# Interleaving three output rows over the quarters of w2, and loading w1's first quarter in two halves

## The chip, the cores and the metric

The kernel runs on one core of one Trainium2 chip. The metric is the time of one execution on the device, in microseconds (us). Three runs of the kernel before gave 223.17, 225.45 and 226.80 us; the median is 225.45 us. One further execution was profiled.

## The reference, cut to what matters

Two blocks follow each other: a linear attention with a decay per head, and a mixer with a low-rank product and a two-layer MLP.

```
gamma = 1.0 - 2.0 ** (-5.0 - np.arange(H))
for t in range(S):
    state = gamma[None, :, None, None] * state + np.einsum('bhd,bhe->bhde', k[:, :, t], v[:, :, t])
    y[:, :, t] = scale * np.einsum('bhd,bhde->bhe', q[:, :, t], state)
...
xt = x.transpose(0, 2, 1)
h = xt @ U @ V
u = x + h.transpose(0, 2, 1)
ch = np.maximum(u @ w_ch1, 0.0) @ w_ch2
return (u + ch)
```

There are 4 batches, 8 heads of 64 values, 768 positions. x, the attention's output with the heads side by side, is 768 x 512 per batch; U is 768 x 32, V 32 x 768, w_ch1 ("w1") 512 x 2048, w_ch2 ("w2") 2048 x 512. Inputs and output are float32; the kernel computes its matrix products in bfloat16.

## The kernel before, in words

**Attention.** A batch's 768 positions are cut into six chunks of 128. For batches 1 to 3 a chunk ci takes these steps: the input tiles of k, q and v are cast (and q and v scaled) to bfloat16 (`prep`, L207, and `prep_q1`, L198); k and q are transposed; `score` (L279) multiplies them into R[ci % 2], a tile of two PSUM banks, and DVE masks both banks (L287); `mix` (L292) multiplies the masked scores with v, adds the product of q with the state so far, ACT evacuates that (x, L308), and the state is brought up to date and evacuated (nsz, L322). Batch 0 has code of its own that runs in two groups of four heads (`STEPS`, L525), an order written out by hand over all engines.

**Mixer.** For each batch, `up` (L425) makes sixteen pieces of relu(u @ w1) for positions 0 to 511, `up_two` (L440) eight pieces for the rest, and `down` (L455) the product with w2: six output rows j of 128 positions, four pieces each (m0 = 0, 4, 8, 12), and a piece needs one quarter of w2. That is 48 pieces in a batch, all counted by the planner at the same cost, 0.864. A row's four pieces add up in one PSUM bank, and after the fourth DVE adds u and the row goes to a store, issued by POOL.

**PSUM.** Eight banks: R[0] and R[1] with two each, one called st, and three called mlp, which are handed out in turn by `bank("mlp")` to whatever asks: an up piece, a down row, a transpose. Who takes a bank waits until the one who had it three calls earlier has been evacuated.

**Order.** `weave` (L486) emits a batch's pieces one after another, and before a piece all the marks whose place (a fraction of the batch's 48 pieces) has come. A mark is a step of the next batch's attention or of a low-rank product: `mark(at, f, ...)` (L798). The places for batch 1 stand in the table AT (L788) and the loop after it. Each engine then runs its own instructions in that order, and an instruction that waits holds up all behind it on its engine. With the places of the kernel before, batch 1's steps fall as follows among batch 0's pieces, counted from 0 (24 is the first down piece, j=0 m0=0):

| before piece | what |
|---|---|
| 23 | `turn_k1` (L255) of chunks 0, 1 |
| 25 | casts of k chunks 2, 3 on ACT; `turn_q1` (L264) of 0, 1 |
| 28 | `score` 0, 1 |
| 29 / 30 | `turn_k1` 2, 3 / `mix` 0 |
| 31 / 32 | `turn_q1` 2, 3 / `mix` 1 |
| 33 | `score` 2, 3 |
| 36 / 37 / 38 | `mix` 2 / `turn_q1` 4, 5 / `mix` 3 |
| 39 | `score` 4, 5 |
| 41 / 43 | `mix` 4 / `mix` 5 |
| 44 / 46 | `lr_proj_turn` (L374) / `lr_uT` (L389) |

`turn_k1` and `turn_q1` transpose on TensorE through an mlp bank; ACT evacuates k, ACT and DVE in turn q. `lr_proj_turn` begins with 24 small products over all six x of the batch, in order of j.

**Loads.** SP issues the loads of k, q and v. POOL issues the weights: w1 in four quarters of 512 columns (`load_w1`, L228), w2 in four quarters (`load_w2`, L233). Both queues share the DMA engines. In the step list, `w0` and `w1` issue w1's first and second quarter; the third is issued after the list (L772), then a tiny copy waits for the first quarter (`feed_behind(511)`, L774) and lets SP go on with q and v of chunks 0 and 1, then w1's last quarter and all four quarters of w2 are issued, and a copy behind w1's second quarter (L779) lets SP go on with chunks 2 to 5. POOL then clears three tiles and casts k, q and v of chunks 0 and 1 (L782).

**The first up pieces.** The step `B1`, `B2` (L742) begins up pieces 0 and 1 with the first two and the third of four rows of w1 (c = 0, 1 and 2), as the transposed u arrives row by row; `up` then adds c = 3.

Of the kernel before, what the change touches and what calls it, by code (L numbers as in the profile page):

```python
# [16 lines left out]
def kernel(  # L17
# [12 lines left out]
    P = 128  # L30
# [193 lines left out]
    def prep_two(nm, pp, eng="P"):  # L224
        for ci in (2 * pp, 2 * pp + 1):
            prep(nm, 1, ci, eng)

    def load_w1(lo, n):  # L228
        nc.gpsimd.dma_start(
            out=w1b[:, :, ds(lo, n)],  # L230
            in_=moe_w_ch1[:, ds(lo, n)].rearrange("(c p) n -> p c n", p=P))

    def load_w2(j):  # L233
        nc.gpsimd.dma_start(
# [20 lines left out]
    def turn_k1(ci):  # L255
        t = bts["k", 1, ci] = rpre.tile([P, 4, P], bf16, tag="kT", name=f"kT_1_{ci}",
                                        bufs=3)
        tp = bank("mlp")
        for hp in range(4):
            nc.tensor.matmul(tp[:, ts(hp, P)], pre["k", 1, ci][:, ds(2 * hp, 2)], ident,  # L260
                             start=True, stop=True)
        evac("A", t.rearrange("p n m -> p (n m)"), tp)

    def turn_q1(ci):  # L264
        g, pp = ci % 2, ci // 2
        if g == 0:
            t = rpre.tile([P, 4, 2 * P], bf16, tag="qT1", name=f"qT_1_{pp}", bufs=2)
            bts["q", 1, ci], bts["q", 1, ci + 1] = t[:, :, :P], t[:, :, P:]
            bts["q1", pp] = t
        src, t = pre.pop(("q", 1, ci)), bts["q1", pp]  # L270
        tp = bank("mlp")
        for n in range(2):
            for j in range(2):
                nc.tensor.matmul(tp[:, ts(2 * n + j, P)], src[:, j, ds(2 * n, 2)], ident,
                                 start=True, stop=True)
        evac("AD"[g], t[:, ds(2 * g, 2)].rearrange("p n (t j) -> p n j t", j=2),
             tp.rearrange("p (n j t) -> p n j t", n=2, j=2))
# [135 lines left out]
    def mlp_pieces(b):  # L413
        gT = gtp.tile([P, NM, S], bf16, tag="gT", name=f"gT_{b}")
        pieces = []
        n = [0]

        def relu(dst, src):
            n[0] += 1
            if n[0] % 3 == 0:  # L420
                nc.vector.tensor_relu(dst, src)  # L421
            else:
                nc.scalar.activation(dst, src, AF.Relu)  # L423

        def up(m, lo, sz):  # L425
            def f():
                g_p = begun.pop((b, m, lo), None)
                c0 = 3 if g_p is not None else 0
                if not c0:
                    g_p = bank("mlp")  # L430
                for c in range(c0, NCB):
                    nc.tensor.matmul(g_p[:, :sz], w1b[:, c, ts(m, P)],  # L432
                                     uTs[b][:, c, ds(lo, sz)], start=(c == 0),
                                     stop=(c == NCB - 1))
                relu(gT[:, m, ds(lo, sz)], g_p[:, :sz])
            return f

        for m in range(NM):
            pieces.append((0.864, up(m, 0, LO)))
        def up_two(m):  # L440
            def f():
                g_p = bank("mlp")
                for n in range(2):
                    for c in range(NCB):
                        nc.tensor.matmul(g_p[:, ts(n, S - LO)], w1b[:, c, ts(m + n, P)],  # L445
                                         uTs[b][:, c, LO:], start=(c == 0),
                                         stop=(c == NCB - 1))
                relu(gT[:, ds(m, 2), LO:], g_p.rearrange("p (n t) -> p n t", n=2))
            return f

        for m in range(0, NM, 2):
            pieces.append((0.864, up_two(m)))
        hold = {}

        def down(j, m0, n0=0, nn=DM):  # L455
            def f():
                if m0 == 0:
                    hold[j, n0] = bank("mlp")
                ch = hold[j, n0]
                for m in range(m0, m0 + 4):  # L460
                    nc.tensor.matmul(ch[:, :nn], gT[:, m, ts(j, P)],  # L461
                                     w2b[:, m, ds(n0, nn)],
                                     start=(m == 0), stop=(m == NM - 1))
                if m0 == NM - 4:
                    o_sb = outp.tile([P, DM], fp32, tag="o_sb",
                                     name=f"o_{b}_{j}_{n0}")[:, :nn]
                    n = ds(n0, nn)
                    nc.vector.tensor_tensor(o_sb, ch[:, :nn], us[b][:, j, n],  # L468
                                            op=ALU.add)
                    if (b, j) == (B - 1, NCK - 1):  # L470
                        nc.sync.dma_start(out=out[b, ts(j, P), n], in_=o_sb)
                    else:
                        stores.append((nc.gpsimd, out[b, ts(j, P), n], o_sb))
            return f

        for j in range(NCK):
            if (b, j) == (B - 1, NCK - 1):
                for n0, nn in ((0, 384), (384, 128)):
                    for m0 in range(0, NM, 4):
                        pieces.append((0.864 * nn / DM, down(j, m0, n0, nn)))  # L480
                continue
            for m0 in range(0, NM, 4):
                pieces.append((0.864, down(j, m0)))
        return pieces
# [204 lines left out]
    def step(s):  # L689
# [15 lines left out]
        if nm in ("K", "Q", "V"):  # L705
            if eng == "S":
                cast_unit("v", u, "P", 0, 2)
            else:
                cast_unit(nm.lower(), u, eng)
        elif nm == "W":  # L710
            cast_unit("v", u, "D", 2, 2)
        elif nm in ("Tk", "Tq"):
            turn_unit(nm[1], u)
        elif nm in ("kT", "qT"):
            turned_unit(nm[0], u, eng)
        elif nm == "S":
            score_unit(u)
        elif nm == "m":
            mask_unit(u)
        elif nm == "ST":  # L720
            state_unit(u, int(at[2]))
        elif nm == "s":
            state_out(u, int(at[2]), eng)
        elif nm == "M":
            mix_unit(u)
        elif nm == "N":
            query_unit(u, False)
        elif nm == "x":
            x_out(u, eng)
        elif nm == "Ub":  # L730
            evac("A", Ub, Uf)
        elif nm == "xt":
            x_turn(u)
        elif nm == "P":
            proj(u, range(NCK if u == 0 else 4))
        elif nm == "R":
            proj(1, range(4, NCK))
        elif nm == "pc":
            pc_out(u // 2, BY["pc"][u // 2])
        elif nm == "E":  # L740
            expand((0, 1) if u == 0 else (u,))
        elif nm == "B":  # L742
            for m in range(2):
                begin_up(m, (0, 1) if u == 1 else (2,))
        elif nm == "u":
            evac(eng, uTs[0][:, u, :LO], xT[u][:, :LO])
        elif nm == "w":
            if u == 0:
                nc.gpsimd.tensor_copy(out=gate0, in_=ready["q", 5][:1, :1])
            load_w1(512 * u, 512)  # L750
        else:
            raise ValueError(s)

# [15 lines left out]

    n_open[0] = 2  # L770
    feed_more()
    load_w1(1024, 512)  # L772
    n_open[0] = 6
    feed_behind(511)  # L774
    n_open[0] = 3 * NCK
    load_w1(1536, 512)
    for j in range(4):
        load_w2(j)
    feed_behind(1023)  # L779
    for t in nsz:  # L780
        nc.gpsimd.memset(t, 0.0)
    for nm in "kqv":  # L782
        prep_two(nm, 0)

    AT = {1: ((0.565, 0.685, 0.80), None, (0.045, 0.09), (0.10, 0.045), None),  # L788
          2: (0.215, 0.185, (0.05, 0.095), (-0.03, 0.0, 0.05, 0.12, 0.39, 0.45),
              (-0.07, -0.035, 0.0, 0.045, 0.36, 0.42)),  # L790
          3: (0.20, 0.20, (0.05, 0.095), (0.01, 0.055, 0.21, 0.255, 0.41, 0.455),
# [13 lines left out]
    for b in range(1, B):  # L805
        s0, step, dm, dt, at_prep = AT[b]
        for ci in range(NCK):
            pair_at = b - 1 + (s0[ci // 2] if b == 1 else s0 + step * (ci // 2))
            if b == 1:
                if ci < NCK - 2:  # L810
                    mark(pair_at - dt[0], turn_k1, ci)
                else:
                    mark(0.671, turn_dma, "k", b, ci)
                mark(pair_at - dt[1], turn_q1, ci)
            else:
                mark(b - 1 + at_prep[ci], prep_chunk, b, ci)
                mark(b - 1 + dt[ci], turn_chunk, b, ci)
            mark(pair_at, score, b, ci)
            mark(pair_at + dm[ci % 2], mix, b, ci)
        if b == 1:  # L820
            for nm, eng, at in (("k", "AP", (0.51, 0.635)), ("q", "PP", (0.54, 0.67)),
                                ("v", "PP", (0.58, 0.70))):
                for pp in (1, 2):
                    mark(at[pp - 1], prep_two, nm, pp, eng[pp - 1])
            mark(0.905, lr_open, b)
            mark(0.905, lr_proj_turn, b)
            mark(0.94, lr_uT, b)
            mark(1.11, lr_expand, b, 0, 4)
        else:
            l0, l1, l2, l3 = LR  # L830
# [43 lines left out]
```

## Time and profile before

| | us |
|---|---|
| median of three runs (lowest, highest) | 225.45 (223.17, 226.80) |
| the profiled execution's own time | 224.14 |
| its span in the trace | 222.3 |
| PE (TensorE matmul) busy | 213.4 (96%) |
| DVE / ACT / POOL busy | 96.7 / 80.7 / 79.7 |
| DMA, queue of SP / of POOL, share of 16 engines | 51.0% / 18.6% |

The span covers the recorded instructions; the execution's own time is 1.84 us longer. PE is busy in nearly the whole span, and the TensorE clock that was granted was 0.998 of full speed. Times below are places in the span. Batch 0's attention and low-rank product fill the first 25 us, its up pieces go from 26 to 49 us, its down pieces with batch 1's attention between them from 49 to 79.5 us.

### The profile page before, as it was taken

How to read it: one execution, taken by the hardware profiler on the slowest of the kernel's cores; microseconds unless marked ns; L12 is line 12 of the kernel's file. 1: busy time of each engine (PE TensorE's matmuls, PEld its weight loads, DVE VectorE, ACT ScalarE, POOL GpSimd, SP SyncE). 2: the span in 40 equal slices, each digit the busy share in tenths (PEclk: the TensorE clock that was granted, in tenths of full speed). 3: DMA queues.
4: the chain of work that ended last, by engine and by line, in shares of the span. 5: the costliest groups of instructions: out<-in, count | busy, mean ns of one | idle time of the engine just before them, and what ended most of it. 6: DMA issues, size and time to landing. Idle time of an engine off the chain costs nothing.

```text
span 222.3 us, 4695 instructions
## 1 busy us (share of the span) xinstructions
PE 213.4 (96%) x1940; PEld 121.9 (55%) x1966; DVE 96.7 (43%) x137; ACT 80.7 (36%) x154; POOL 79.7 (36%) x114
## 2 busy tenths in 40 slices
PE   7999799998999999999999999999999999999993
PEld 2567344774655544578454444587454444774442
DVE  6678546225465176526336144443525242222121
ACT  3676264453734134565030034746030044430000
POOL 5588383012980496036100498053101000000110
PEclk9999999999999999999999999999999999999999
DMA  5999999997899995389899745399113450001212
GB/s 168 330 294 235 192 198 205 195 205 195 214 248 272 272 234 116 75 191 167 181 284 275 182 121 95 82 262 108 47 50 95 141 97 2 0 3 47 92 49 94
DMA packets 91556, 35.10 MB, mean 158 GB/s; under 512 B 73392, under 2 KB 90032, under 8 KB 91536
## 3 DMA queue, kind: packets, MB, share of 16 engines
q1 hardware_dynamic: 85472, 24.59, 51.0%
q0 software_dynamic: 6064, 10.23, 18.6%
q8 instruction: 15, 0.25, 0.5%
q14 instruction: 5, 0.04, 0.1%
HBM read 27.46 MB, written 6.29 MB: 152 GB/s over the span
## 4 chain that ended last, share of the span: by engine, by line
PE 74%; DMA 15%; SPq 7%; issue 1%; POOL 1%; ACT 1%; DVE 0%
PE mlp L461 36%; PE mlp L432 19%; PE mlp L445 10%; DMA in<-in_q_dram 7%; DMA in<-in_k_dram 5%; SPq L106 5%; DMA w1b<-in_moe_w_ch_dram 4%; PE r L284 2%; PE r L305 2%; PE st L316 2%; PE r L300 2%; SPq L137 1%; PE r L347 1%; POOL qp L83 0%; PE r L385 0%
## 5 line engine op out<-in xcount | busy, mean ns | idle before, releaser
L461 PE MATMUL mlp<-w2b,gT 128*128 128x512 bf16 (+2 forms) x384 | 85.9, 370 | 0.9 <-issue 0.2
L423 ACT ACTIVATE gT<-mlp 128x512 bf16<-128x512 f32 x64 | 38.1, 597 | 72.2 <-PE mlp L432 59.1
L461 PEld LDWEIGHTS <-gT 128*128 128x128 bf16 x400 | 37.0, 98 | 39.0 <-issue 0.2
L432 PE MATMUL mlp<-uT,w1b 128*128 128x512 bf16 x244 | 56.3, 379 | 0.3
L411 POOL DMA_DIRECT2D out_dram<-o x23 | 12.8, 556 | 86.8 <-DVE o L468 81.0
L421 DVE TENSOR_SCALAR gT<-mlp 128x512 bf16<-128x512 f32 x32 | 22.1, 689 | 43.5 <-PE mlp L432 22.8
L432 PEld LDWEIGHTS <-w1b 128*128 128x128 bf16 x250 | 23.6, 98 | 27.2
L468 DVE TENSOR_TENSOR o<-mlp,u 128x512 f32<-128x512 f32 (+2 forms) x25 | 16.7, 670 | 44.5 <-PE mlp L461 43.8
L445 PE MATMUL mlp<-uT,w1b 128*128 128x256 bf16 x256 | 29.4, 273 | 0.2 <-ACT gT L423 0.2
L445 PEld LDWEIGHTS <-w1b 128*128 128x128 bf16 x256 | 24.8, 98 | 4.2 <-issue 0.4
L287 DVE TENSOR_TENSOR a<-r,mask 128x1024 bf16<-128x1024 f32 x18 | 21.2, 1219 | 9.5 <-PE r L284 9.5
L83 POOL TENSOR_TENSOR vd<-in,gk 128x512 bf16<-128x512 f32 x18 | 18.7, 1042 | 12.5 <-DMA in<-in_v_dram 7.7
L70 ACT ACTIVATE x<-r 128x512 bf16<-128x512 f32 x20 | 11.9, 596 | 27.3 <-PE r L305 27.0
L81 POOL CAST kd<-in 128x512 bf16<-128x512 f32 x16 | 9.7, 613 | 19.3 <-DMA in<-in_k_dram 19.3
L354 DVE TENSOR_TENSOR u<-r,x 128x512 bf16<-128x512 f32 (+1 forms) x16 | 14.5, 951 | 4.6 <-PE r L347 4.6
L83 POOL TENSOR_TENSOR qd<-in,gq 128x512 bf16<-128x512 f32 x12 | 12.5, 1042 | 1.4 <-DMA in<-in_q_dram 1.4
L70 ACT ACTIVATE nsz<-st 64x256 bf16<-64x256 f32 x30 | 11.2, 372 | 0.3
L83 POOL TENSOR_TENSOR qp<-in,gq 128x512 bf16<-128x512 f32 x6 | 6.2, 1052 | 6.9 <-DMA in<-in_q_dram 6.8
L594 DVE TENSOR_TENSOR a<-r,mask 128x1024 bf16<-128x1024 f32 x6 | 7.3, 1221 | 2.6 <-PE r L587 2.6
L305 PE MATMUL r<-vd,a 128*128 128x64 bf16 x144 | 7.1, 193 | 0.0
L305 PEld LDWEIGHTS <-a 128*128 128x128 bf16 x144 | 6.0, 98 | 0.7
L284 PEld LDWEIGHTS <-kT 64*128 64x128 bf16 x144 | 4.1, 94 | 3.9 <-issue 3.7
(109 smaller groups left out, 147.7 us busy)
## 6 DMA issues: line engine op xcount, KB each, us to landing
in<-in_k_dram SPq DMA_DIRECT2D x24, 256.0 KB, 4.5
in<-in_q_dram SPq DMA_DIRECT2D x24, 256.0 KB, 4.4
in<-in_v_dram SPq DMA_DIRECT2D x24, 256.0 KB, 4.7
out_dram<-o POOLq DMA_DIRECT2D x23, 256.0 KB, 2.5
w1b<-in_moe_w_ch_dram POOLq DMA_DIRECT2D x4, 512.0 KB, 9.2
w2b<-in_moe_w_ch_dram POOLq DMA_DIRECT2D x4, 512.0 KB, 17.2
kT<-kd SPq DMA_TRANSPOSE x14, 3.7
uT<-u SPq DMA_TRANSPOSE x14, 2.4
```

What stands on the lines that cost most here:

```text
L70: nc.scalar.activation(dst, src, AF.Copy)
L83: e.tensor_tensor(dst, src, scale, op=ALU.mult)
L287: nc.vector.tensor_tensor(a, r.rearrange("p i (n m) -> p i n m", n=4), mask[:, None, None, :].to_broadcast([P, 2, 4, P]), op=ALU.mult)
L305: nc.tensor.matmul(o[:, ts(h, D)], a[:, i, hp], vb[:, h], start=(ci == 0 and h == 0), stop=True, skip_group_check=True)
L354: nc.vector.tensor_tensor(v4(us[b][:, ds(j0, nj), e]), R[g][:, :, :nj * P].rearrange("p c (j e) -> p c j e", j=nj), v4(xs[b][:, ds(j0, nj) ...
L411: eng.dma_start(out=dst, in_=src)
L421: nc.vector.tensor_relu(dst, src)
L423: nc.scalar.activation(dst, src, AF.Relu)
L432: nc.tensor.matmul(g_p[:, :sz], w1b[:, c, ts(m, P)], uTs[b][:, c, ds(lo, sz)], start=(c == 0), stop=(c == NCB - 1))
L445: nc.tensor.matmul(g_p[:, ts(n, S - LO)], w1b[:, c, ts(m + n, P)], uTs[b][:, c, LO:], start=(c == 0), stop=(c == NCB - 1))
L461: nc.tensor.matmul(ch[:, :nn], gT[:, m, ts(j, P)], w2b[:, m, ds(n0, nn)], start=(m == 0), stop=(m == NM - 1))
L468: nc.vector.tensor_tensor(o_sb, ch[:, :nn], us[b][:, j, n], op=ALU.add)
```

## The change

Four things are changed, and the marks are placed anew.

- Batch 0's first three output rows run side by side: j = 0, 1, 2 at m0 = 0, then the three at m0 = 4, and so on. The later rows and the other batches keep their order. Each of the three holds an mlp bank until the fourth quarter.
- `turn_k1` and `turn_q1` use the second bank of R[ci % 2] in place of an mlp bank.
- w1's first quarter is loaded in two halves (rows c = 0, 1 and c = 2, 3) at the places of `w0` and `w1` in the step list; the second quarter is issued after the list, ahead of the third. The steps `B1`, `B2` begin three up pieces in place of two.
- w2's last quarter is issued behind the cast of v's chunk 0.

```
-    def load_w1(lo, n):
+    def load_w1(lo, n, c=0, nc_=NCB):
         nc.gpsimd.dma_start(
-            out=w1b[:, :, ds(lo, n)],
-            in_=moe_w_ch1[:, ds(lo, n)].rearrange("(c p) n -> p c n", p=P))
+            out=w1b[:, ds(c, nc_), ds(lo, n)],
+            in_=moe_w_ch1[ds(P * c, P * nc_), ds(lo, n)].rearrange(
+                "(c p) n -> p c n", p=P))
...
     def turn_k1(ci):
-        tp = bank("mlp")
+        tp = R[ci % 2][:, 1]
...
     def turn_q1(ci):
-        tp = bank("mlp")
+        tp = R[g][:, 1]
...
-        for j in range(NCK):
+        side = 3 if b == 0 else 1
+        for m0 in range(0, NM, 4):
+            pieces += [(0.864, down(j, m0)) for j in range(side)]
+        for j in range(side, NCK):
...
         elif nm == "B":
-            for m in range(2):
+            for m in range(3):
                 begin_up(m, (0, 1) if u == 1 else (2,))
...
-            load_w1(512 * u, 512)
+            load_w1(0, 512, 2 * u, 2)
...
     n_open[0] = 2
     feed_more()
+    load_w1(512, 512)
     load_w1(1024, 512)
...
-    for j in range(4):
+    for j in range(3):
         load_w2(j)
     feed_behind(1023)
...
-    for nm in "kqv":
+    for nm in "kq":
         prep_two(nm, 0)
+    prep("v", 1, 0)
+    load_w2(3)
+    prep("v", 1, 1)
...
-    AT = {1: ((0.565, 0.685, 0.80), None, (0.045, 0.09), (0.10, 0.045), None),
+    AT = {1: ((0.565, 0.69, 0.81), None, (0.045, 0.09),
+              (0.465, 0.465, 0.63, 0.642, None, None, 0.52, 0.52, 0.662, 0.662, 0.78, 0.78),
+              None),
...
-                    mark(pair_at - dt[0], turn_k1, ci)
+                    mark(dt[ci], turn_k1, ci)
...
-                mark(pair_at - dt[1], turn_q1, ci)
+                mark(dt[NCK + ci], turn_q1, ci)
...
-            for nm, eng, at in (("k", "AP", (0.51, 0.635)), ("q", "PP", (0.54, 0.67)),
+            for nm, eng, at in (("k", "AP", (0.535, 0.635)), ("q", "PP", (0.54, 0.67)),
...
-            mark(0.905, lr_open, b)
-            mark(0.905, lr_proj_turn, b)
-            mark(0.94, lr_uT, b)
+            mark(0.915, lr_open, b)
+            mark(0.915, lr_proj_turn, b)
+            mark(0.948, lr_uT, b)
```

With the new places the table above becomes: the casts of k chunks 2, 3 on ACT come before piece 26, behind `turn_q1` 0, 1; `turn_k1` 2, 3 before piece 31; `mix` 1 and then `turn_q1` 2, 3 before piece 32; `score` 2, 3 before piece 34; `mix` 3 and right after it `turn_q1` 4, 5 before piece 38; `mix` 4 before piece 42; `mix` 5 and right after it `lr_proj_turn` before piece 44. The others stay where they were.

## The prediction, on record before the result

> **What bounds the kernel now.** I read the page first, then TensorE's waits, then the busy time by stretch, then the timelines of TensorE and ACT around the waits, and last the weight queue in windows of 1 us.
>
> The page, part 1, engines:
> ```profile
> PE 213.4 (96%) x1940; PEld 121.9 (55%) x1966; DVE 96.7 (43%) x137; ACT 80.7 (36%) x154; POOL 79.7 (36%) x114
> ```
> The waits of PE:
> ```profile
> PE mlp L756 <- DVE zeros L152: 1.2, 1, 1.2
> PE mlp L403 <- DMA w1b<-in_moe_w_ch_dram: 1.1, 1, 1.1
> ...
> PE r L284 <- ACT qT L70: 0.5, 1, 0.5
> PE mlp L445 <- ACT gT L423: 0.2, 1, 0.2
> ```
> Busy time by stretch (stretch, its length, then PE and PEld busy, and so on), cut at these waits:
> ```profile
> 24.97:26.05 1.08, 0.00 (x2) 0.01 (x1) 1.04 (x2) 0.00 (x0) 0.00 (x0) 1.00 1.20 198
> 26.05:47.81 21.76, 21.66 (x158) 12.87 (x161) 8.54 (x12) 10.17 (x17) 9.62 (x15) 1.00 1.20 201
> 47.81:48.05 0.24, 0.00 (x1) 0.00 (x0) 0.00 (x0) 0.24 (x2) 0.00 (x0) 1.00 1.22 250
> 48.05:52.99 4.94, 4.88 (x31) 2.77 (x32) 1.43 (x2) 2.36 (x5) 1.04 (x1) 1.00 0.76 191
> 52.99:53.50 0.51, 0.00 (x1) 0.02 (x2) 0.48 (x1) 0.46 (x1) 0.00 (x0) 1.00 1.20 287
> ```
> The reader is to see that TensorE is the bound from 25 us to the end. In the stretch that the change touches it stands still three times: 1.08 us before the first up piece (for w1's first quarter), 0.24 us at the last up piece (an mlp bank whose relu is not out), 0.51 us before score 0. Their sum, 1.83 us, is all that this execution has to give; the work on TensorE is the same before and after. Why score 0 waits stands in ACT's timeline (start, length):
> ```profile
> 51.36 0.63 ACT L77 ACTIVATE kd<-in 128x512 bf16<-128x512 f32 x1 [2.38 <-DMA in<-in_k_dram]
> 52.19 0.63 ACT L77 ACTIVATE kd<-in 128x512 bf16<-128x512 f32 x1 [0.20 <-DMA in<-in_k_dram]
> 52.72 0.72 ACT L70 ACTIVATE qT<-mlp 128x512 bf16<-128x512 f32 x1
> ...
> 56.67 0.60 ACT L70 ACTIVATE x<-r 128x512 bf16<-128x512 f32 x1 [0.17 <-PE r L305]
> 57.16 0.77 ACT L70 ACTIVATE nsz<-st 64x256 bf16<-64x256 f32 x2
> 57.98 0.75 ACT L70 ACTIVATE qT<-mlp 128x512 bf16<-128x512 f32 x1
> ```
> q's evacuation stands behind two casts that wait for k's loads of chunks 2 and 3.
>
> **w1's first quarter in two, a third piece begun.** The weight queue (q0), windows 20:21, 23:24 and 25:26 (packets, MB):
> ```profile
> q0 software_dynamic: 44, 0.05, 57.8%
> ...
> q0 software_dynamic: 168, 0.16, 121.8%
> ...
> q0 software_dynamic: 192, 0.19, 117.7%
> ```
> With the windows between (0.16, 0.17, 0.19) the queue has moved 0.5 MB, one quarter, at about 23.8 us; the first quarter landed at 26.0 (issue 18.05 plus 8.0), so 2.2 us behind. The second landed at 28.5 (19.53 plus 9.0), 2.1 us behind its own 1.0 MB. A first half (0.25 MB at about 22.2) should land near 24.4. TensorE is done with the step before at 24.97, and both evacuations on ACT end at 24.44, so B1 starts at 25.00: a gain of 1.05 us. Its six matmuls (0.216 us each, from 0.86 for four) end at 26.30; the second half, at 26.0, is then there.
>
> A late wait follows it. Piece 3 takes piece 0's bank. B2 (three) ends at 26.95, pieces 0 to 2 need one matmul each and the expansion 0.23: 27.82. Relu 0 starts 0.19 after its matmul's end (27.16, the distance seen before), takes 0.60, and 0.06 passes to TensorE: 28.01. A new wait of 0.19. Net here: -0.86. From both sides: -1.3 at most (the six matmuls of B1 run inside the wait if all w1 is late), and +0.2 if the first half lands no sooner than the quarter does.
>
> w1's second quarter goes from 19.53 to 21.30 in POOL's stream: it is moved past the cast of v5 (1.06). It is needed at piece 4, at 28.87 by the sum above. In the queue's order it stands behind the same bytes as before, and these run out at 23.8; from issue to first packet the first quarter took 2.3 us (18.05 to about 20.4), so the second has packets from 23.6. I take 28.5, no wait. The other end: it lands later by the whole 1.77, at 30.3, a wait of 1.5. The third quarter's issue moves from 21.30 to about 22.1; it stands behind the same bytes and landed at 31.4, needed at 33: nothing. The copy that lets SP go on still waits for the landing at 26.0.
>
> One rule of the Trainium skill speaks against the halves: "DMA: Bandwidth & Descriptors", section "Anatomy of one DMA — SWDGE (gpsimd) path", gives each DMA a fixed cost of about 2 us, most of it the receipt of the last byte. If the halves paid it one after the other, the second would land near 28 us, B2 would wait 1.7 us, and the whole sum would come to about +1.3. The second quarter, landing 2.5 us behind the first at 0.2 MB in a us, shows no such addition; the rival by it is worked out from rows below.
>
> **The turns in R.** The mlp bank that the last up piece waited for is no longer taken by a turn: -0.24. The turns need R free: chunks 2 and 3 turn before piece 31, a mix and a piece behind the masks of 0 and 1 (1.22 each, done before mix 0 and 1): nothing. If the cover were gone, a mask is 1.22. During pieces 24 to 35 no other step asks for an mlp bank; the fourth row takes row 0's, whose add (0.69) is done 2 us earlier.
>
> **The casts of k on ACT behind qT.** They leave qT's way: score 0, now at about 51.5 in place of 53.5, finds q evacuated at 49.5: -0.51. The casts still end at 52.8; next on ACT is x of mix 0, at about 54.3, and turn_k1 2 needs them at 55.3: 1.5 and 2.5 us of cover.
>
> **w2's last quarter.** POOL issues it behind the cast of v 0 (landed 44.6, cast to 45.7); it is moved past a gate, three clears, two casts of k, two of q and one of v, and 0.77 us of issue goes ahead of v 1's cast, which waits for its load until 50.3 anyway. The queue is still at w2's third quarter then (landed 46.9), so it lands at 50 to 52; first needed at piece 33, near 58.6. Nothing; 6 us of cover. The loads of k, q, v share the engines with it for as long as before. q 2 and 3 are cast by 57.1, and turn_q1 3 comes at about 57.5: 0.4 us of cover, then us for us (taken 0, ends -0 and +0.7, by the 1.1 that a late first packet could shift).
>
> **Two steps set closer.** Mix 3 is now followed at once by turn_q1 4, 5, one piece and score 4. On ACT, from mix 0 above: 1.69 us from mix's L305 (56.24) to the end of nsz (57.93), then q's evacuation, 0.70, and 0.06. TensorE gets from L305 to score in 0.23 + 0.22 + 0.45 + 0.86 = 1.76, ACT in 2.45: +0.69 (0 to 0.9). Mix 5 is followed at once by lr_proj_turn: x needs 0.80 from the end of L305 and 0.06, the products of rows 0 to 4 take 5/6 of 0.45: +0.49 (0 to 0.6). Score 2: mask 2 starts behind row 0's add, ending at about 61.6 where mix 2 comes at 61.8: 0 (to 0.3).
>
> Three stores come together, on POOL behind the casts of q and v 4, 5 (about 65.8, landing 2.5 later), with three output buffers: row 3's add, at 68.4, just finds one. An add held up there costs nothing until its bank is wanted five pieces on.
>
> **Sum.** -0.86 - 0.24 - 0.51 + 0.69 + 0.49 = -0.43 us. On the profiled execution, 224.14 (span 222.3 and 1.84 around it), that is 223.7. That execution lies 1.3 below the median, 225.45, between the lowest and the highest; the three runs lie 3.6 us apart, so 2% (4.5 us) is about what a measurement of this kernel can tell from no change.
>
> **Rivals.**
> - w1's second quarter is late and TensorE waits at piece 4: 1.5 us, net +1.05, 225.2. This is the one on the other side; it decides from a landing after 29.3 (28.87 plus 0.43). For it: only 0.2 us of bytes are left in the queue when its packets come. Against: the queue has bytes. 0.17.
> - The second half pays a fixed part of its own: the smallest transfer in the list of DMA issues (64 KB) takes 1.6 us, so 27.6 and a wait of 1.3 in B2: net +0.87, 225.0. Against: the spacing of the quarters. 0.08. By the Trainium skill's figure its wait would be 1.7.
> - The first half lands no sooner than the whole: the halving doesn't do what it says, net +0.6, 224.8. Against: the queue is in order. 0.10.
> - The two new waits on ACT are hidden: net -1.6, 222.5. For: both rest on distances of 0.06 to 0.2 us read from one execution. 0.13.
> - q's loads late for turn_q1 3, 0.7 of wait: 224.4. 0.07.
> - Over 2% slower: several waits at once, above all w1 or q by 4 us and more: 0.07. Over 2% faster: 1.83 us of waits do not hold 4.5; only if the median's runs wait more for loads than the profiled one: 0.05.
>
> **How the numbers follow.** My forecast has 0.33. Its own range is 223 to 224.6. With the rivals, 222.5 to 225.2, and the spread of the runs around them (223.17 to 226.80 before) the range is 221.8 to 226.7. All cases but the last two lie within 2% of 225.45: 0.88 the same, 0.05 faster, 0.07 slower.
>
> **What would show it.** Right: B1 starting near 25.0 with no wait on w1b, no wait at L445 and at score 0, new waits of PE on ACT qT at score 4 and on ACT x at the products of lr_proj_turn, and a relu's bank at piece 3. Wrong: a wait on w1b at L432 (piece 4), on w1b at B2, on POOL qp at a turn, or a longer stretch between 80 us and the end, which the change should leave at its length.

## The result, and the profile after

The changed kernel takes 225.49 us (median of 20 runs, 223.89 to 228.53), the kernel before 224.10 us (20 runs). The ratio is 1.0063, with a 95% interval of 1.0041 to 1.0085: about 1.4 us slower, within the 2% either way. The forecast was 223.7 us, 0.43 us less than the profiled execution of the kernel before, so the sign was wrong.

The first profile of the changed kernel fell in a disturbed execution (227.84 us); the readings below are from a second one, 225.56 us with a span of 223.8, called as_changed. Its page, engines:

```profile
PE 215.9 (96%) x1966; PEld 122.2 (55%) x1966; DVE 96.5 (43%) x137; ACT 80.6 (36%) x154; POOL 80.6 (36%) x115
```
The waits of its PE:
```profile
PE mlp L433 <- DMA w1b<-in_moe_w_ch_dram: 1.4, 1, 1.4
...
PE r L275 <- ACT x L70: 0.5, 2, 0.2
PE mlp L379 <- ACT x L70: 0.3, 1, 0.3
...
PE r L285 <- ACT qT L70: 0.2, 1, 0.2
```
The three waits that the prediction counted (w1 before the first up piece, gT at the last, qT at score 0) are gone. In their place stand w1 again, now at up piece 4 (L433), x twice at a turn of q (L275), x at lr_proj_turn (L379), and qT at a later score. Busy time by stretch (stretch, length, PE, PEld and so on), cut at the first up matmul, piece 4, the first down piece, score 0 and batch 1's first up piece:

```profile
25.03:28.87 3.84, 3.84 (x26) 1.51 (x24) 2.33 (x4) 1.09 (x2) 3.03 (x5) 1.00 1.11 172
28.87:30.43 1.56, 0.20 (x2) 0.01 (x1) 0.85 (x2) 0.60 (x1) 0.06 (x1) 1.00 1.20 209
30.43:49.12 18.69, 18.69 (x145) 11.99 (x145) 6.41 (x8) 9.20 (x16) 7.41 (x11) 1.00 1.12 198
49.12:53.11 3.99, 3.99 (x26) 1.92 (x23) 1.42 (x2) 2.19 (x4) 0.18 (x1) 1.00 1.11 198
53.11:80.95 27.84, 26.74 (x286) 15.57 (x285) 13.12 (x15) 10.37 (x21) 16.68 (x21) 1.00 1.04 252
```
B1 starts at 25.03 (the forecast said 25.00), but TensorE stands still from 28.87 to 30.43. The last stretch, from score 0 to batch 1's first up piece, takes 27.84 us. The same stretch in the profile before:

```profile
53.50:79.51 26.01, 25.75 (x280) 15.17 (x285) 12.84 (x15) 10.39 (x21) 15.62 (x20) 1.00 1.00 244
```
It took 26.01 us there, 1.83 less.

The best tool of this study came out of this: TensorE's timeline, cut at five fixed points. Each stretch has the same work in every version, so its length differs by waits alone. All numbers are start times from that timeline, or differences of them, in us. (lr_turn is the first transpose of batch 0's u among the up pieces, L368 before and L369 after; lines of the changed kernel lie one to five further down.)

| profile | B1 starts | B1 to lr_turn | to first down piece | to score 0 | to batch 1's first up | rest |
|---|---|---|---|---|---|---|
| before, as shown | 26.05 | 4.65 | 18.22 | 4.58 | 26.01 | 142.8 |
| before_look | 26.45 | 4.66 | 18.21 | 4.49 | 26.01 | 142.9 |
| before_look2 | 26.00 | 4.79 | 18.21 | 4.00 | 26.00 | 142.9 |
| before_look3 | 25.39 | 4.66 | 18.22 | 4.01 | 26.01 | 142.9 |
| as_changed | 25.03 | 6.27 | 17.82 | 3.99 | 27.84 | 142.9 |
| changed_look | 25.06 | 5.57 | 17.82 | 4.00 | 27.83 | 142.9 |

Two columns hardly move between executions of one kernel but differ between the two kernels: to the first down piece (-0.40 with the change) and from score 0 on (+1.83). The rest, behind the change, hardly moves at all. The three others move with loads.

### The profile page after: what moved, and what is told of

Read it like the earlier page. It is cut to its first block, busy times and chain, and to the rows that moved or that the text cites. A ratio compares the mean times of both kernels' runs of the same rounds, so it can differ in the third digit from the quotient of the medians.

```text
span 226.1 us, 4699 instructions
## 1 busy us (share of the span) xinstructions
PE 215.0 (95%) x1940; PEld 123.1 (54%) x1966; DVE 96.8 (43%) x137; ACT 80.6 (36%) x154; POOL 80.3 (36%) x115
## 4 chain that ended last, share of the span: by engine, by line
PE 83%; DMA 7%; SPq 4%; ACT 2%; issue 2%; POOL 1%; DVE 0%; POOLq 0%; ACTq 0%
PE mlp L462 36%; PE mlp L433 23%; PE mlp L446 12%; SPq L106 4%; DMA w1b<-in_moe_w_ch_dram 4%; DMA in<-in_k_dram 3%; PE r L285 2%; PE r L306 2%; PE r L301 2%; PE st L317 1%; PE r L348 1%; PE mlp L566 1%; ACT x L70 1%; PE mlp L583 0%; POOL ku L83 0%
## 5 line engine op out<-in xcount | busy, mean ns | idle before, releaser
L433 PE MATMUL mlp<-uT,w1b 128*128 128x512 bf16 x241 | 55.9, 379 | 0.9 <-DMA w1b<-in_moe_w_ch_dram 0.6
L433 PEld LDWEIGHTS <-w1b 128*128 128x128 bf16 x247 | 23.2, 98 | 27.9 <-DMA w1b<-in_moe_w_ch_dram 1.1
L81 POOL CAST kd<-in 128x512 bf16<-128x512 f32 x16 | 9.7, 610 | 20.7 <-DMA in<-in_k_dram 19.1
L301 PEld LDWEIGHTS <-qT 128*128 128x128 bf16 x60 | 4.6, 98 | 3.0 <-issue 0.4
```

Source lines behind the costliest of these rows:

```text
L433: nc.tensor.matmul(g_p[:, :sz], w1b[:, c, ts(m, P)], uTs[b][:, c, ds(lo, sz)], start=(c == 0), stop=(c == NCB - 1))
```

## The experiments

Three theories were to be told apart. A: steps set too close lose the time, between score 0 and batch 1. B: w1's second quarter, issued later, loses it at piece 4. C: both. Gains and losses below are the ratio to the kernel before on the same chip, times 223.5 us.

**as_changed** is the changed kernel as it is.

> The changed kernel once more, for a profile and for the size of the loss. It should be about 1.4 us slower than before (0.6%). Theory A (steps set too close): down pieces to batch 1's first up piece, 30.6 us before, take about 1.2 us longer, with waits of TensorE at the second turn of q in pairs 1 and 2 (0.4 each), at score 4 (0.35) and at the first products of lr_proj_turn (0.4). Theory B (w1's order): TensorE waits 0.6 us or more at up piece 4 for w1's second quarter, and the stretch from the first up piece to the first down piece is longer than before by that.

Ratio 1.0068 (1.0033 to 1.0104), +1.5 us. Both places lost time in the one profile, so A and B each had its wait. The two turns show how A's waits come about. TensorE's timeline:

```profile
56.73 0.61 PE L261 MATMUL r<-ident,kd 128*128 128x128 bf16 x8
57.17 1.03 PE L462 MATMUL mlp<-w2b,gT 128*128 128x512 bf16 x4
58.34 0.38 PE L301 MATMUL r<-nsz,qT 128*128 128x128 bf16 x4
...
59.02 0.39 PE L275 MATMUL r<-ident,qp 128*128 128x128 bf16 x4
59.65 0.38 PE L275 MATMUL r<-ident,qp 128*128 128x128 bf16 x4 [0.24 <-ACT x L70]
```
and ACT's:
```profile
57.21 1.09 ACT L70 ACTIVATE kT<-r 128x512 bf16<-128x512 f32 x2
59.00 0.60 ACT L70 ACTIVATE x<-r 128x512 bf16<-128x512 f32 x1 [0.70 <-PE r L306]
```
Four transposes take 0.22 us, so the second turn could start at 59.24; it starts at 59.65, 0.05 behind the end of x of mix 1 (59.60). That x is read from bank 0 of R[1] and the turn goes to bank 1, but they are one tile, and TensorE waits for the tile. In the same way mix 1 (L301) could start at 58.03 and starts at 58.34, 0.04 behind k's evacuation (58.30), which reads the other bank of R[1]. The view names 0.24 where 0.41 is lost: a matmul's modelled end lies some 0.17 behind the time at which the next could start. The last loss of this kind is at lr_proj_turn, whose products of the sixth x wait for that x. Its products and the next step in as_changed, and then in the kernel before:

```profile
75.23 0.46 PE L379 MATMUL mlp<-x,Ub 128*32 128x128 bf16 x20
75.99 0.24 PE L379 MATMUL mlp<-x,Ub 128*32 128x128 bf16 x4 [0.29 <-ACT x L70]
76.16 1.07 PE L386 MATMUL r<-ident,x 128*128 128x128 bf16 x16
```
```profile
74.26 0.52 PE L378 MATMUL mlp<-x,Ub 128*32 128x128 bf16 x24
74.72 1.07 PE L385 MATMUL r<-ident,x 128*128 128x128 bf16 x16
```
The products take 0.93 us up to the next step, where they took 0.46: 0.47 is lost. Summed by start times: 0.31 at mix 1, 0.41 at each second turn of pairs 1 and 2, 0.25 more than before at score 4 and 0.47 here. That is 1.85, the whole of the 1.83 within rounding.

**w1_as_before** and **w1_alone** split the change. The first undoes w1's part:

```
-            for m in range(3):
+            for m in range(2):
-            load_w1(0, 512, 2 * u, 2)
+            load_w1(512 * u, 512)
-    load_w1(512, 512)
```


> The changed kernel with w1 loaded as before (whole quarters, the second in its old place, two pieces begun); all else changed. Theory A: the loss stays, +1.2 us or more against before (+2 if the halves brought the 0.86 that I reckoned). Theory B: the loss is gone, within 0.3 us of before or faster.

1.0057 (1.0027 to 1.0087), +1.3 us: the loss stays, against B, and undoing w1's part changed the time by no more than 0.1 to 0.2 us. Its profile has 17.82 to the first down piece and 27.84 from score 0, as the changed kernel. The second makes the same edit the other way round, in the kernel before:

> The kernel before with w1's first quarter in halves, its second quarter behind them and three pieces begun; nothing else. Theory A: no slower than before, 0 to 0.9 us faster. Theory B: 0.5 us slower or more, with a wait on w1 at up piece 4.

1.0029 (0.9993 to 1.0065): no change that can be told. In its profile B1 starts at 24.63, and piece 4 doesn't wait (4.74 from B1 to lr_turn); but score 0 waits 0.68 for qT, which stands behind k's casts and their loads on ACT; the profile before showed 0.51. In this one profile a part of what was gained ahead of that load is given back at it.

**q_r0_marks_back** takes the close steps apart: one call turns both q of a pair, 

```
+        for g in range(2):
+            ...
+                    nc.tensor.matmul(R[0][:, g, ts(2 * n + j, P)], src[:, j, ds(2 * n, 2)],
+                                     ident, start=True, stop=True)
+        for g in range(2):
+            evac("AD"[g], ..., R[0][:, g]...)
-    AT = {1: ((0.565, 0.69, 0.81) ... 0.662, 0.662, 0.78, 0.78),
+    AT = {1: ((0.565, 0.69, 0.80) ... 0.662, 0.662, 0.755, 0.755),
-            mark(0.915, lr_proj_turn, b)
+            mark(0.905, lr_proj_turn, b)
```


> The changed kernel with the close steps taken apart: both turns of q of a pair go into the two banks of R[0], their matmuls ahead of both evacuations, so the second turn waits for no x; and score 4, 5, turn_q1 4, 5, mix 4, 5 and lr_proj_turn stand at their old places. Theory A: 1.3 to 1.6 us faster than the changed kernel, so equal to before or up to 0.4 us faster. Theory B: no more than 0.4 us faster than the changed kernel.

1.0028 (0.9993 to 1.0062), +0.6: 0.9 better than the changed kernel, where A had 1.3 to 1.6. From score 0 it takes 26.86, so 0.98 of the 1.83 is gone, the waits on x among it. By start times 0.31 at mix 1 and 0.55 at score 2 are left, and the one at score 2 is new:

```profile
PE r L286 <- DVE qT L72: 0.5, 1, 0.5
```
```profile
60.72 0.74 ACT L70 ACTIVATE qT<-r 128x512 bf16<-128x512 f32 x1
```
```profile
61.49 0.73 DVE L72 CAST qT<-r 128x512 bf16<-128x512 f32 x1 [5.15 <-ACT qT L70]
```
DVE's evacuation of one bank of R[0] now starts when ACT's of the other ends (61.46); in as_changed, from two tiles, they ran side by side. The profile also waits 1.1 us at piece 4 (5.86 from B1 to lr_turn).

**q2_early**, **marks_open** and the two together mend one cause each.

```
             load_w1(0, 512, 2 * u, 2)
+            if u == 1:
+                load_w1(512, 512)
...
-    load_w1(512, 512)
```


> The changed kernel with w1's second quarter issued right behind the second half, ahead of v5's cast, as early as before; all else changed. Theory C (both causes, from the second profile of the changed kernel: 1.56 us at up piece 4, and 1.8 us more between score 0 and batch 1's first up piece): the wait at piece 4 goes, B1 still starts near 25.0, so 1.2 to 1.6 us faster than the changed kernel, within 0.4 us of before. Theory A (the marks alone count): no more than 0.4 us faster than the changed kernel. v5's cast comes 0.75 us later; if the products with v5 wait for it, up to 0.5 of the gain is lost.

1.0052 (1.0026 to 1.0077), +1.2. Its profile does what C said (B1 at 24.95, 4.74 to lr_turn, no wait at piece 4), but the runs gained 0.3, as A said. The profiled execution lost 1.0 us in batch 2:

```profile
PE mlp L433 <- DMA uT<-u: 1.0, 1, 1.0
```
a wait that no other profile has; it stands in one execution and doesn't explain the median.

marks_open sets the marks a piece apart:

```
-    AT = {1: ((0.565, 0.69, 0.81) ... 0.662, 0.662, 0.78, 0.78),
+    AT = {1: ((0.565, 0.69, 0.80) ... 0.67, 0.67, 0.755, 0.755),
-            mark(0.915, lr_proj_turn, b)
-            mark(0.948, lr_uT, b)
+            mark(0.905, lr_proj_turn, b)
+            mark(0.94, lr_uT, b)
```


> The changed kernel with the close steps one piece apart (turn_q1 2, 3 a piece behind mix 1; turn_q1 4, 5, score 4, 5, mix 4, 5 and lr_proj_turn at their old places), w1 as changed. Theory C: the waits at the two turns (0.41 each), score 4 (0.25) and the first products of lr_proj_turn (0.38) go, the one at mix 1 (0.31, for k's evacuation from the same R) stays: 1.3 to 1.5 us faster than the changed kernel. Theory B (w1's order alone): no more than 0.4 us faster.

1.0025 (0.9997 to 1.0052), +0.6: 0.95 better than the changed kernel, where theory C had 1.3 to 1.5, and 26.45 us from score 0 (1.39 less). Its profile has no wait at piece 4 (4.74 from B1 to lr_turn), though w1 is loaded as in the changed kernel.

> Both mends together. Theory C: the two add up, 2.5 to 3 us faster than the changed kernel, 1.0 to 1.5 us faster than before. If one wait only takes the other's place (the turns of q coming before their loads, for one), no faster than before.

0.9995 (0.9966 to 1.0025): 1.6 better than the changed kernel, equal to before. The 2.5 to 3 us of the forecast weren't there.

**q2_early_on_before** and **q2_late_on_before** try w1's order on the kernel before: halves with the second quarter right behind, and the whole first quarter with the second issued after the step list.

> The kernel before with w1's first quarter in halves, three pieces begun, and the second quarter issued right behind the second half; nothing else. Theory C: 0.5 to 1.0 us faster than before (B1 near 25.0, no wait at piece 4), less what score 0 then waits longer for k's loads (it waited 0.51 before and comes 1 us earlier): if that takes all, no faster, 0 to 0.3.

1.0010 (0.9976 to 1.0043): no gain, though B1 starts at 24.93 in its profile. There the second half landed only at 26.4, 2.5 us behind the first, B2 waited 0.26 for it (5.00 from B1 to lr_turn), and score 0 came 0.6 late.

> The kernel before with only w1's second quarter issued later: behind v5's cast, in its place after the step list; the first quarter whole, two pieces begun. If issue sets the landing (about 8.3 us after it, by the profiles so far), it lands near 29.7 or later where piece 4 comes at 29.8: 0.2 to 0.8 us slower than before, with a wait at piece 4. If the order in the queue sets it, no change.

0.9999 (0.9964 to 1.0035). In its profile B1 itself starts late, at 26.90, so piece 4 comes late as well and finds its quarter. This didn't test the issue's delay as it was meant to.

**before_look, before_look2, before_look3 and changed_look** ask what differs between executions.

> The kernel before once more, for a second profile: how far its waits vary between executions. If the wait before the first up piece (1.08 us in the profile shown) is its usual one, B1 starts near 26 again; if the usual execution has less of it, B1 starts near 25 and halving w1's first quarter has little to give.

> The changed kernel once more, for a third profile: the waits at the turns of q (0.41 twice), mix 1, score 4 and lr_proj_turn should stand as in the second profile; the wait at up piece 4 may lie anywhere between 0 and 1.6 us, by when v5's load lets POOL issue w1's second quarter.

> The kernel before, a third profile. If the waits before B1 and score 0 belong to loads, their lengths differ again (1.08 and 0.77 before B1 so far) while the stretches between stay: 4.65, 18.2, 26.0 and 142.9 us.

> The kernel before, a fourth profile, for the same question: the waits before B1 and before score 0 in one more execution, and the same stretches between them.

The table above has them. PE's waits in before_look3 on w1 and at the last up piece:

```profile
PE mlp L403 <- DMA w1b<-in_moe_w_ch_dram: 0.4, 1, 0.4
PE mlp L445 <- ACT gT L423: 0.2, 1, 0.2
```
The wait on w1 before the first up piece is 1.08, 0.77, 0.38 and none in the four profiles of before; score 0 waits in two of the four and not at all in the others. The changed kernel waits at piece 4 in all three of its profiles: its stretch from B1 is 5.54 (in the first one), 6.27 and 5.57 where 4.74 is the least. (In changed_look the view puts this wait down to a relu on ACT; but piece 4 starts at 29.76, and POOL's copy of the second quarter, which waits for the landing, at 29.77.) Of the three other versions with w1 in the same order, q_r0_marks_back waits there and w1_alone and marks_open don't.

**w1_as_before_marks_open, all_apart and all_apart_q2_early** look for a version that pays. The first is marks_open with w1 as before.

> The changed kernel with both mended the plain way: w1 loaded as before (two pieces begun), the close steps one piece apart. If the loss is the close steps and w1's late second quarter, it should be 0.4 to 0.9 us faster than before (the waits at the last up piece and at score 0 gone, 0.31 at mix 1 added), and equal to the version with the second quarter issued early. If the three rows side by side, the turns in R or w2's late quarter cost something of their own, it is no faster than before.

1.0022 (0.9992 to 1.0053): the expected gain of 0.4 to 0.9 us over the kernel before isn't there. In all_apart w1 is as before too, and each step of batch 1 comes at least a piece behind the one it waits for:

```
-    AT = {1: ((0.565, 0.69, 0.81) ... 0.662, 0.662, 0.78, 0.78),
+    AT = {1: ((0.565, 0.71, 0.815) ... 0.69, 0.69, 0.775, 0.775),
-            mark(pair_at + dm[ci % 2], mix, b, ci)
+            mark((0.61, 0.68, 0.755, 0.80, 0.855, 0.905)[ci] if b == 1 else ...
-            mark(0.915, lr_proj_turn, b)
+            mark(0.93, lr_proj_turn, b)
```


> The three rows side by side, the turns in R and w2's late quarter kept; w1 as before; every step of batch 1 at least a piece behind the one it waits for (mix 1 two pieces behind turn_k1 3 too). Theory C: from score 0 to batch 1's first up piece 26.0 us as before, 17.8 between turn and the first down piece: 0.4 us faster than before, and up to 1.0 where the kernel before waits at score 0. If one of the three parts kept costs something of its own, no faster than before.

1.0034 (0.9997 to 1.0071): not the 0.4 us faster that was expected. Its profile has no wait of PE on anything of batch 1 that the view lists, but 26.45 us from score 0, not 26.0: small gaps (0.23 at mix 4, 0.12 at mix 3 and 0.08 within score 2) eat the 0.41 won at the last up piece.

> The same with w1's first quarter in halves and the second issued right behind. Theory C: as all_apart, and 0 to 0.9 us faster still by the wait before B1, if the kernel before usually has it.

1.0006 (0.9973 to 1.0039). No version measurably beat the kernel before.

## Why the prediction was wrong, point by point

**What fits all runs.** Take from each profile only what is fixed: +0.09 for three begun pieces (4.74 against 4.65), -0.40 at the last up piece, and the length from score 0 less 26.01. No load is in it.

| version | fixed part, us | measured, us (95%) |
|---|---|---|
| changed (20 runs each) | +1.5 | +1.4 (0.9 to 1.9) |
| w1_as_before | +1.4 | +1.3 (0.6 to 1.9) |
| q2_early | +1.5 | +1.2 (0.6 to 1.7) |
| q_r0_marks_back | +0.5 | +0.6 (-0.2 to 1.4) |
| marks_open | +0.1 | +0.6 (-0.1 to 1.2) |
| w1_as_before_marks_open | 0.0 | +0.5 (-0.2 to 1.2) |
| all_apart | 0.0 | +0.8 (-0.1 to 1.6) |
| all_apart_q2_early | +0.2 | +0.1 (-0.6 to 0.9) |
| q2_early_marks_open | +0.1 | -0.1 (-0.8 to 0.6) |
| w1_alone | +0.1 | +0.7 (-0.2 to 1.5) |
| q2_early_on_before | +0.1 | +0.2 (-0.5 to 1.0) |
| q2_late_on_before | 0.0 | 0.0 (-0.8 to 0.8) |

All twelve lie within their intervals. The three versions with the steps close lie clear of no change, and none of the nine others does. So A was right in the main: the loss against the kernel before is shown to be the steps set too close. Theory C fell in its size: mending w1's order took away the wait at piece 4 but gave 0.3, not 1.2 to 1.6.

**Where forecast and measurement part.** They are 1.8 us apart (-0.43 and +1.4). The terms of the sum that are engine on engine (the late wait at piece 3, the last up piece, the two close steps) made +1.13; by the table they came to +1.5, 0.4 more. The terms that are waits on loads (1.05 before the first up piece, 0.51 before score 0) made -1.56; what the runs leave for them, +1.4 less +1.5, is about nothing, with an interval of 0.5 either way. So 1.18 of the loss was forecast, as the two close steps; what turned the sign is the gain that didn't come. Two steps failed: the bigger one took the load waits of one profile for what the change has to give, the smaller one put the turns in R at nothing.

**The smaller step that failed: "The turns need R free ... nothing".** I looked only for who had R ahead of a turn, and at the bank, not at the tile. By the tile, turn_q1 3 waits for x of mix 1 (0.41) and mix 1 for k's turn (0.31): 0.72 us that the sum had at nothing.

**The two steps set closer** were priced well. Score 4: 0.69 forecast, and 0.66 came (0.41 already at turn_q1 5, 0.25 at the score). lr_proj_turn: 0.49 forecast, 0.47 came. That the score 2 chain would not wait was right. The late wait at piece 3, 0.19 in the sum, came as 0.09.

**The last up piece** gave 0.41 in place of 0.24: the view's number is short by the modelled end.

**The bigger step that failed: "all that this execution has to give" taken as the gain.** The first half landed at 24.5 (forecast 24.4), the second at 25.7 (26.0), and B1 started at 25.03 (25.00): the mechanism was right. The halves land 1.2 us apart here, so the fixed cost of about 2 us that the Trainium skill's page "DMA: Bandwidth & Descriptors" gives each DMA (section "Anatomy of one DMA — SWDGE (gpsimd) path") didn't come one behind the other in this profile. But 1.05 is no gain of the usual execution: the wait that it removes was 1.08 in the profile I read, and 0.56 in the mean of four. In the profiles of w1_as_before, w1_as_before_marks_open and all_apart, which load w1 as before, it is 0.29 once and none twice. The same holds for score 0, which I put at 0.51: the mean of four is 0.27 above the least. The runs agree: the interval of w1_alone, -0.2 to +1.5, doesn't reach the -0.86 that the sum had for this part.

**w1's second quarter: "I take 28.5, no wait".** In as_changed it landed at 30.4, near the other end that I had worked out (30.3); the wait was 1.56. POOL's timeline and the weight queue (21:22, 23:24, 24:25, 25:26) in as_changed:

```profile
20.69 1.04 POOL L83 TENSOR_TENSOR vu<-in,gk 128x512 bf16<-128x512 f32 x1 [0.22 <-DMA in<-in_v_dram]
21.69 1.55 POOL L229 DMA_DIRECT2D w1b<-in_moe_w_ch_dram  x2
```
```profile
q0 software_dynamic: 131, 0.13, 98.2%
...
q0 software_dynamic: 159, 0.16, 114.2%
q0 software_dynamic: 113, 0.11, 102.3%
q0 software_dynamic: 139, 0.14, 97.4%
```
The second quarter is issued behind v5's cast, which may wait for its load (0.22 here, 0.53 in changed_look, 0.92 in q_r0_marks_back), and in as_changed the queue moves 0.11 and 0.14 MB in the windows from 24 to 26, where it moved 0.19 and 0.19 before. So the queue did run low between the halves and the second quarter; "the same bytes ahead" was not enough. But in marks_open, with w1 in the same order, v5's cast doesn't wait for its load and POOL issues the quarter at 20.8:

```profile
19.79 1.06 POOL L83 TENSOR_TENSOR vu<-in,gk 128x512 bf16<-128x512 f32 x1
20.79 1.56 POOL L229 DMA_DIRECT2D w1b<-in_moe_w_ch_dram  x2
```
There it landed at 28.4, as forecast, and piece 4 didn't wait; w1_alone is alike (issued at 20.7, landed at 28.5). In marks_open too the queue ran low (0.11 and 0.10 MB from 23 to 25), so in these profiles it is the time of issue that tells: the landing comes 7.6 to 8.7 us behind it in all five (as_changed, changed_look, q_r0_marks_back, marks_open, w1_alone). The rival that I gave 0.17 is what three of the five show, at 0.8 to 1.5 us, and two don't; the mean is 0.70. That it costs the median as much is not shown: q2_early removed it and gained 0.3. By the profiles, w1's part and score 0 together come out near even: 0.83 gained (0.56 and 0.27), 0.70 lost at piece 4.

**w2's last quarter** was right at nothing: no profile of the changed kernel waits on w2b.

**What stays open.** The versions with the steps apart measured 0.5 to 0.8 us behind their fixed part in three of five cases, inside their intervals; a small cost of its own, or of loads, can't be excluded. The two that aren't behind are the two with w1's second quarter issued right behind the halves; whether that order is the reason isn't shown, for on the kernel before it gained nothing. The profiles of the three also take 0.2 to 0.5 us longer behind the last matmul, where the last store runs; that is one profile each. Whether the late second quarter alone costs the median anything wasn't settled.

## What to carry to other kernels

A wait on a load in one profile is a draw, not a price: take two or three profiles before counting its removal as a gain, and count only the waits of engine on engine with no load in the chain behind them, which repeated to 0.01 us here. The wait of score 0 on ACT looked like one of these, but k's loads stood behind it. When two steps share a tile, ask who waits for the whole tile, not for the half that is used. And when a kernel is bound by one engine with a fixed order, cut its timeline at fixed points: each stretch then shows its own loss.

## What was not expected

Stretches of TensorE's timeline came back almost exactly in the four profiles of the kernel before (18.21 and 18.22; 26.00 and 26.01; 142.8 and 142.9), while the first 25 us, which hang on loads, moved by a microsecond (B1 from 25.39 to 26.45). Over all versions the last of these stretches lay between 142.8 and 143.4 us, but for one of 144.0, and B1 moved by more than 2 us. So the profiles of one kernel differ mostly ahead of B1 and at the waits on loads behind it. That the spread of 4 us between the runs arises there too is likely, but not shown: most runs left no trace.
